# Regrouping the last group of modes alone in a fused linear-attention and spectral-mixing kernel

## The chip, the cores and the metric

The kernel runs on one core of one Trainium2 chip, as one launch. The metric is the device time of an execution in microseconds (us). Of three timed executions the median was 444.92 us (444.81, 444.92 and 445.96).

## What is computed

Two layers run one behind the other. The first is a linear attention (8 batches, 8 heads, 576 positions, head width 64) with exponential features; its result, laid out as `x` with 8 batches, 576 positions and 512 columns, feeds the second. Only the second matters for the change:

```python
X = np.fft.rfft(x, axis=1)
Xr, Xi = np.real(X[:, :64]), np.imag(X[:, :64])
Yr = einsum('bmd,mde->bme', Xr, w_r) - einsum('bmd,mde->bme', Xi, w_i)
Yi = einsum('bmd,mde->bme', Xr, w_i) + einsum('bmd,mde->bme', Xi, w_r)
y = np.fft.irfft(Yr + 1j * Yi, n=576, axis=1)   # the other frequencies are 0
u = x + y
out = u + np.maximum(u @ w_ch, 0)
```

Each of the 64 lowest frequencies (modes) has its own two 512 x 512 matrices, 134 MB in all as they stand in memory. They are read once.

## The kernel before, in words

**Stages.** For the first 310 us the attention runs, one step per batch and pair of heads, and the mode products of three quarters of the columns run between its steps. A *group* `k` (0 to 31) is a set of modes by a set of the 512 input columns. Groups 24 to 31 are the last 128 input columns; group 24+gi holds eight modes, 4·gi to 4·gi+3 and 32 above these. From group 21 on the work is in the loop that begins at line 858, the *last stage*, and everything the change touches lies there.

**Weights.** `weights(k)` issues four transfers per group from the POOL queue (line 169): two halves of `wr`, two of `wi`, 512 KB written each. A group's tiles are one of three sets (`NW = 3`), so group 31 is loaded into the tiles of group 28, once group 28 has been multiplied.

**One group in the loop** (lines 859 to 880). TensorE (PE) multiplies by `wr` (`modes_of(k, 0)`, line 438), does a piece of other work, and multiplies by `wi` (`modes_of(k, 1)`), both into one PSUM tile `psY`. VectorE (DVE) adds the sum of the earlier columns out of `Yacc` and gives `yst` (line 466): 128 rows, which are 8 modes by real and imaginary part by 8 batches. PE transposes it (line 837), DVE copies the transpose into one half of `sY` (line 838). `sY` has two halves, for an even and an odd `gi`.

**The regrouping.** The inverse transform needs, for each batch, the mode rows of that batch. When both halves of `sY` are there, `by_batch(sY, P)` picks with a column step of 8 the 32 columns of each batch: `mm_z` multiplies them by `w_ch` (line 732), `mm_r` by a unit matrix (line 738), four batches side by side in four quarters of the PE. Batches 0 to 3 go into the PSUM tile T0 and 4 to 7 into T1. Eight copies of 32 rows then put them into `zall` and `yall` (one tile, `zy`), four by ScalarE (ACT) out of T0 and four by DVE out of T1 (line 748). They are queued in a list; `regroup(n)` issues the next n pairs: two pairs at once, the other two in the next group behind its first piece of other work. Pair P fills the rows 32·P to 32·P+31 of every batch.

**The other work.** Every 128 x 512 piece of `x` is transposed (`flip_x`, line 694, copied by DVE in line 697) and multiplied by `w_ch` (`times_w`, line 705): two PSUM tiles `psW` per call, each cast by ACT into `xw` (line 707). The tag of `psW` has two buffers. Some pieces of `x` are also put into another row order (`reordered`, lines 722 and 724), through the tiles T0 and T1.

**Groups 30 and 31 before the change.** Group 30 (gi = 6) fills the even half of the last `sY` and then runs a `flip_x` and the next to last `times_w` calls. Behind the loop stand a `times_w`, the first half of group 31, the last `times_w`, `add_xw` of the first output unit, the second half of group 31, `add_x`, and then `mode_sum` in two halves. `yst` of both groups goes to `yall` by three transfers (line 893). The transposes fill the odd half of `sY`; `mm_r` for batches 0 to 3 gives batch 0's `yall` rows by a DVE copy (line 903). `mm_z` for batches 0 to 3 gives batch 0's `zall` rows by an ACT copy (line 908) and a staging tile `st0` (line 909); `mm_z` for batches 4 to 7 gives `st1`, copied by DVE. Seven transfers bring the other batches' `zall` rows from there (line 913).

**Output units.** 18 units then follow (lines 915 to 929). Each adds on PE `xw` (778) and the inverse transform of `zall` (785) into `psB`, which ACT passes through the maximum (787), and `x` (793) and the inverse transform of `yall` (799) into `psA`, which DVE adds (801). Ten units have `x` added on POOL instead (804). SP sends each out (929). PSUM tiles of odd units come from a new pool that takes the place of the stage's own.

The order of instructions on each engine is that of the program text (`tc.manual_schedule()`); engines wait for one another by semaphores.

Of the kernel before, what the change touches and what calls it, by code (L numbers as in the profile page):

```python
# [10 lines left out]
F32 = mybir.dt.float32  # L11
F32R = mybir.dt.float32r
BF16 = mybir.dt.bfloat16
# [5 lines left out]
B_, H_, S_, D_ = 8, 8, 576, 64  # L19
NMODES = 64  # L20
DMODEL = 512
# [5 lines left out]
def kernel(  # L27
# [11 lines left out]
    nc = tc.nc  # L39
# [4 lines left out]
    psum = psum_cm.__enter__()  # L44
    pw = ctx.enter_context(tc.tile_pool(name="pw", bufs=3))

    ident_b = const.tile([128, 128], BF16, name="ident_b")
# [9 lines left out]
    wchb = pers.tile([128, 4, DMODEL], BF16, name="wchb")  # L57
# [49 lines left out]

    groups = [(h, -1 - G) for h in range(2) for G in range(4)]
    groups += [(g, gi) for g in range(1, 4) for gi in range(8)]

    after = [3] * 4 + [7] * 4 + [15] * 8 + [23] * 8 + [31] * 8
    W = {}
# [333 lines left out]
    def mode_sum(k, psY, pb=None):  # L446
        g, gi = groups[k]
        if gi < 0:
            G = -1 - gi
            if g == 0:  # L450
                nc.vector.tensor_copy(Yacc[:, 2 * G:2 * G + 2, :], psY)
            else:
                nc.vector.tensor_tensor(  # L453
                    out=Yacc[:, 2 * G:2 * G + 2, :], in0=psY, in1=Yacc[:, 2 * G:2 * G + 2, :],
                    op=ALU.add)
        elif g < 3:
            nc.vector.tensor_tensor(
                out=Yacc[:, gi, :], in0=psY, in1=Yacc[:, gi, :], op=ALU.add)
        else:

            cuts = [0, DMODEL] if k < 31 else [0, DMODEL // 2, DMODEL]
            yst = []
            for a, b in zip(cuts, cuts[1:]):
                t = pb.tile([128, b - a], BF16, name="yst", tag="yst" if k < 31 else f"yst{a}",
                            bufs=2 if k < 31 else 1)
                nc.vector.tensor_tensor(out=t, in0=psY[:, a:b], in1=Yacc[:, gi, a:b], op=ALU.add)
                yst += [t[:, x:x + 128] for x in range(0, b - a, 128)]
                Yst.append((t, gi, a, b))
            return yst
# [201 lines left out]
    pb = ctx.enter_context(tc.tile_pool(name="pb", bufs=2))  # L671
# [3 lines left out]
    psum = psum_cm.__enter__()  # L675

    zy = pb.tile([128, 2, B_ + 1, DMODEL], BF16, name="zy", bufs=1)
    zall, yall = zy[:, 0], zy[:, 1]
    Yst = []
# [6 lines left out]
    def slot(b):  # L686
        return b or B_

    def flip_x():
        i = todo.pop(0)  # L690
        pt = psum.tile([128, 2, 4, 128], BF16, name="pt", tag="tr")
        for x in range(2):
            for dc in range(4):
                nc.tensor.transpose(  # L694
                    pt[:, x, dc, :], xs_all[:, i + x, dc * 128:(dc + 1) * 128], ident_b)
        sT = pb.tile([128, 2, 4, 128], BF16, name="sT", tag="sT", bufs=3)
        nc.vector.tensor_copy(sT, pt)  # L697
        ahead.append((i, sT))

    def times_w():  # L700
        i, sT = ahead.pop(0)
        for x in range(2):
            ps = psum.tile([128, DMODEL], F32, name="psW", tag="pW", bufs=2)
            for dc in range(4):
                nc.tensor.matmul(ps, lhsT=sT[:, x, dc, :], rhs=wchb[:, dc, :],  # L705
                                 start=(dc == 0), stop=(dc == 3))
            nc.scalar.copy(xw[:, i + x - N_EARLY, :], ps)  # L707
# [18 lines left out]
    def columns(sY):  # L726
        return [sY[:, dc].rearrange("p g c -> p (g c)") for dc in range(4)]

    def mm_z(ps, cols, h):
        for dc in range(4):  # L730
            for j in range(4):
                nc.tensor.matmul(ps[32 * j:32 * j + 32, :], lhsT=cols[dc][:, j + 4 * h::8],
                                 rhs=wchb[:, dc, :], start=(dc == 0), stop=(dc == 3))

    def mm_r(ps, cols, h):
        for dc in range(4):
            for j in range(4):
                nc.tensor.matmul(
                    ps[32 * j:32 * j + 32, dc * 128:(dc + 1) * 128],
                    lhsT=cols[dc][:, j + 4 * h::8], rhs=ident_b, start=True, stop=True)  # L740
# [15 lines left out]
    def regroup(n):  # L756
        for _ in range(n):
            if copies:
                copies.pop(0)()
# [71 lines left out]
                        ap=[[9 * DMODEL, 64], [5 * DMODEL, 2], [1, m * DMODEL]]),  # L831
                o[:, s, :].rearrange("p c e -> p (c e)")))

    def transposed(yst, sY, gi, pts):
        for (a, b), pt in pts:
            for dc in range(a, b):
                nc.tensor.transpose(pt[:, dc - a, :], yst[dc], ident_b)
            nc.vector.tensor_copy(sY[:, a:b, gi % 2, :], pt)

    def modes_of(k, part, psY=None):  # L840
        if part == 0:
            while issue["k"] < min(k + NW, 32):
                weights(issue["k"])
                issue["k"] += 1
            issue_weights()
        return mode_mm(k, "pY", (part,), psY)

    def piece():
        times_w()
        if todo:  # L850
            flip_x()

    issue = dict(k=k_in)
    pieces_behind = (22, 24, 26, 28, 30)
    with tc.manual_schedule():
        flip_x()
        flip_x()
        for k in range(k_out, 31):
            gi = groups[k][1]
            psY = modes_of(k, 0)  # L860
            piece()
            regroup(99)
            modes_of(k, 1, psY)
            yst = mode_sum(k, psY, pb)
            if k in pieces_behind:
                times_w()
            if yst is not None:
                if gi % 2 == 0:
                    sY = pb.tile([128, 4, 2, 128], BF16, name="sY", tag="sY")
                transposed(yst, sY, gi, (((0, 4), psum.tile([128, 4, 128], BF16, name="ptY",  # L870
                                                            tag="tr")),))
            if k in pieces_behind and todo:
                flip_x()
            if yst is not None and gi % 2 == 1:
                by_batch(sY, gi // 2)
                regroup(2)
            else:
                for tag in ("T0", "T1"):
                    if reorder:
                        reordered(tag)  # L880
        assert not todo and not copies and not reorder
        times_w()
        psY = modes_of(31, 0)
        times_w()
        assert not ahead
        u0 = units[0]
        add_xw(u0)
        modes_of(31, 1, psY)
        add_x(u0)
        yst = mode_sum(31, psY, pb)  # L890
        for m, eng in ((-2, nc.sync), (-1, nc.gpsimd), (-3, nc.sync)):
            t, gi, a, b = Yst[m]
            eng.dma_start(yall[96 + 16 * (gi - 6):112 + 16 * (gi - 6), 0:B_, a:b],
                          t)
        transposed(yst, sY, 7, [
            (dcs, psum.tile([128, 2, 128], BF16, name="ptY", tag=tag, bufs=bufs))
            for dcs, tag, bufs in (((0, 2), "tr", 1), ((2, 4), "pW", 2))])
        cols = columns(sY)
        st = [pb.tile([128, DMODEL], BF16, name=f"st{h}", bufs=1) for h in range(2)]
        rows = slice(96, 128)  # L900
        r = psum.tile([128, DMODEL], F32, name="psR", tag="tr")
        mm_r(r, cols, 0)
        nc.vector.tensor_copy(yall[rows, slot(0), :], r[0:32])
        for h in range(2):
            z = psum.tile([128, DMODEL], F32, name="psZ", tag=("pW", "pY")[h], bufs=2 - h)
            mm_z(z, cols, h)
            if h == 0:
                nc.scalar.copy(zall[rows, slot(0), :], z[0:32])
            (nc.scalar.copy, nc.vector.tensor_copy)[h](st[h], z)
        for b, eng in ((1, nc.sync), (4, nc.gpsimd), (5, nc.sync), (6, nc.gpsimd),  # L910
                       (2, nc.sync), (7, nc.gpsimd), (3, nc.gpsimd)):
            j = b % 4
            eng.dma_start(zall[rows, b, :], st[b // 4][32 * j:32 * j + 32])

        for n, u in enumerate(units):
            if n == 1:
                psum_cm.__exit__(None, None, None)
                psum = ctx.enter_context(
                    tc.tile_pool(name="psumT", bufs=1, space=bass.MemoryType.PSUM))
            output_tile(u)  # L920
            if n:
                add_xw(u)
            add_z(u)
            if n:
                add_x(u)
            spec(u)
            while leave and leave[0] <= n:
                for dst, part in units[leave.pop(0)]["dmas"]:
                    nc.sync.dma_start(dst, part)
# [30 lines left out]
```

## Time and profile before

| | |
|---|---|
| median of three executions | 444.92 us |
| profiled execution | 445.59 us |
| its span, first to last instruction | 443.8 us |
| mean granted TensorE clock | 0.879 |
| PE busy | 310.9 us (70%) |
| DVE busy | 293.7 us (66%) |
| ACT busy | 270.8 us (61%) |
| moved by the DMA engines | 97.86 MB, 221 GB/s on average |

A row of the timeline gives the start in us from the span's start, the duration in us, the engine, the line, the operation, the tile written and the tiles read, their sizes and how many instructions are merged in the row; in brackets stands the idle time before it and what ended it. PE is a matrix product, PEld the load of its stationary operand; `128*32` says that a stationary operand of 128 rows and 32 columns takes one quarter of the array. A row of the chain of waits gives the start, the duration and what the end of the program was waiting for in that stretch. A row of the table by stretches gives, for each stretch, the busy time of each engine with its number of instructions, the granted clock (1.00 is full), the busy share of the DMA engines and GB/s.

### The profile page before, as it was taken

The page shows a single profiled execution, that of the slowest core. Times are in us where ns is not written, and L with a number is a line of the kernel's source. Part 1 is how long each engine was busy: PE and PEld are TensorE (multiplying, and loading weights), DVE is VectorE, ACT ScalarE, POOL GpSimd, SP SyncE. Part 2 cuts the span into 40 slices and gives each one's busy share as a digit, 9 for nine tenths or more (in the row PEclk, how much of TensorE's full clock was granted, in tenths as well). Part 3 has the DMA queues.
Part 4 walks back from the last instruction along what each step waited for, and adds up shares of the span by engine and source line. Part 5 has one row for each costly group of instructions (what it writes and reads, how often), then busy time and mean ns, then how long its engine had stood idle before and what let it go on. Part 6 is the DMA issues. An engine that isn't in the chain of part 4 may idle for free.

```text
span 443.8 us, 11840 instructions
## 1 busy us (share of the span) xinstructions
PE 310.9 (70%) x4981; PEld 201.5 (45%) x4981; DVE 293.7 (66%) x417; ACT 270.8 (61%) x567; POOL 218.1 (49%) x303
## 2 busy tenths in 40 slices
PE   0666667775767777677453767766897776789993
PEld 0455555554555655465342544433443333344441
DVE  4778879989888687878744796664232356363783
ACT  3676687886886875688633866663363254353762
POOL 6776448585566656547534554442222222200893
PEclk9999899899896596868966787888999699889997
DMA  8999999999999999999999999999999999993598
GB/s 190 243 228 218 220 228 217 229 218 218 230 221 223 221 233 221 223 233 222 223 220 222 222 222 211 211 212 211 211 211 211 211 211 211 211 207 74 183 363 328
DMA packets 60997, 97.86 MB, mean 221 GB/s; under 512 B 3936, under 2 KB 28992, under 8 KB 60944
## 3 DMA queue, kind: packets, MB, share of 16 engines
q0 software_dynamic: 51952, 76.69, 95.9%
q1 hardware_dynamic: 8832, 20.35, 13.3%
q8 instruction: 39, 0.64, 0.5%
q10 hardware_dynamic: 160, 0.07, 0.1%
q14 instruction: 14, 0.11, 0.1%
HBM read 163.64 MB, written 9.44 MB: 390 GB/s over the span
## 4 chain that ended last, share of the span: by engine, by line
DMA 55%; DVE 18%; PE 14%; issue 4%; ACT 4%; POOL 2%; ACTq 0%; SPq 0%; DVEq 0%; POOLq 0%
DMA wi<-in_moe_w_i_dram 35%; DMA wr<-in_moe_w_r_dram 9%; DMA k<-in_k_dram 8%; DVE mkq L248 7%; DVE nd L337 2%; DVE xs_all L351 2%; ACT AA L255 2%; DVE tB L330 2%; PE psB L785 2%; PE psB L778 2%; DMA kn<-in_k_dram 2%; PE psA L799 2%; PE ptr L199 1%; POOL vaug L285 1%; DMA fs<-in_w_phi_dram 1%
## 5 line engine op out<-in xcount | busy, mean ns | idle before, releaser
L285 POOL TENSOR_TENSOR vaug<-vn,ee 128x576 bf16<-128x576 f32 x64 | 72.7, 1156 | 45.7 <-ACT ee L270 43.6
L255 ACT ACTIVATE AA<-psT 128x1024 bf16<-128x1024 f32 x64 | 62.0, 1021 | 24.9 <-PE psT L223 24.2
L169 POOL DMA_DIRECT2D wr<-in_moe_w_r_dram x48 | 29.7, 620 | 78.4 <-PE psY L438 21.0
L277 ACT ACTIVATE e<-mkq 64x4 f32<-64x4 f32 (+1 forms) x128 | 26.3, 206 | 60.1 <-DVE mkq L248 57.7
L259 ACT ACTIVATE AA<-psk 128x1024 bf16<-128x1024 f32 x64 | 61.4, 1009 | 0.0
L169 POOL DMA_DIRECT2D wi<-in_moe_w_i_dram x48 | 29.9, 625 | 45.0 <-DMA wi<-in_moe_w_i_dram 13.5
L248 DVE TENSOR_REDUCE mkq<-psk 128x8 f32<-128x1024 f32 x32 | 38.7, 1211 | 0.7 <-PE psk L214 0.7
L248 DVE TENSOR_REDUCE mkq<-psq 128x8 f32<-128x1024 f32 x32 | 38.9, 1217 | 0.4 <-PE psq L214 0.3
L438 PE MATMUL psY<-wi,XT 128*32 128x512 bf16 x192 | 19.1, 477 | 26.1 <-DMA wi<-in_moe_w_i_dram 26.1
L707 ACT CAST xw<-psW 128x512 bf16<-128x512 f32 x34 | 19.8, 586 | 25.5 <-PE psW L705 25.2
L438 PEld LDWEIGHTS <-XT 128*32 128x32 bf16 x384 | 14.6, 173 | 45.8 <-issue 23.1
L705 PE MATMUL psW<-wchb,sT 128*128 128x512 bf16 x136 | 33.3, 389 | 0.0
L205 DVE COPY kT<-ptr 128x640 bf16<-128x640 bf16 x32 | 15.7, 492 | 25.3 <-PE ptr L199 25.3
L330 DVE TENSOR_TENSOR tB<-psNB,e 128x650 f32<-128x650 f32 x32 | 26.6, 832 | 8.8 <-PE psNB L320 8.4
L320 PEld LDWEIGHTS <-AA 128*128 128x128 bf16 x640 | 28.8, 110 | 7.6 <-issue 7.1
L697 DVE COPY sT<-pt 128x1024 bf16<-128x1024 bf16 x17 | 11.8, 692 | 30.5 <-PE pt L694 30.5
L223 PE MATMUL psT<-qT,w 64*128 64x512 bf16 x64 | 15.4, 471 | 23.4 <-DVE mkq L248 23.3
L199 PE MATMUL ptr<-ident_b,k 128*128 128x128 bf16 x160 | 18.1, 259 | 19.6 <-DVE qT L205 17.7
L351 DVE TENSOR_TENSOR xs_all<-nd,rden 128x640 bf16<-128x640 f32 x32 | 30.4, 951 | 1.1
L301 PE MATMUL kvz<-vaug,AA 64*128 64x65 bf16 x1152 | 28.8, 208 | 2.3 <-DVE Yacc L453 1.5
L337 DVE TENSOR_TENSOR nd<-psNA,tB 128x650 f32<-128x650 f32 x32 | 26.7, 835 | 3.8 <-DVE tB L330 0.5
L301 PEld LDWEIGHTS <-AA 64*128 64x128 bf16 x1152 | 24.5, 106 | 6.9 <-issue 2.3
(142 smaller groups left out, 726.6 us busy)
## 6 DMA issues: line engine op xcount, KB each, us to landing
wr<-in_moe_w_r_dram POOLq DMA_DIRECT2D x62, 512.0 KB, 18.9
wi<-in_moe_w_i_dram POOLq DMA_DIRECT2D x62, 512.0 KB, 18.7
out_dram<-of SPq DMA_DIRECT2D x15, 512.0 KB, 4.7
vn<-in_v_dram SPq DMA_DIRECT2D x24, 288.0 KB, 6.0
q<-in_q_dram POOLq DMA_DIRECT2D x12, 288.0 KB, 17.4
k<-in_k_dram POOLq DMA_DIRECT2D x12, 288.0 KB, 17.6
vn<-in_v_dram SPq DMA_DIRECT2D x16, 144.0 KB, 7.0
Yacc<-in_moe_w_r_dram POOLq DMA_DIRECT2D x2, 512.0 KB, 8.7
```

The lines of the kernel that those rows point to most:

```text
L169: nc.gpsimd.dma_start(t.rearrange("p (m i) e -> p m (i e)", i=2), w[8 * gi + y:8 * gi + 8:2, g * 128:(g + 1) * 128, :].rearrange("m (p i) ...
L248: nc.vector.tensor_reduce(out=o, in_=i, axis=AX.X, op=ALU.max, apply_absolute_value=True)
L255: nc.scalar.activation(AA[:, 0, ab, 0:1024].rearrange("f (x j p) -> f j x p", j=2, p=64), st["psT"].rearrange("f j (x p) -> f j x p", p=64 ...
L259: nc.scalar.activation(AA[:, 1, ab, 0:1024].rearrange("p (c j f) -> p j c f", c=4, j=2), st["psk"], ACT.Exp, scale=sc)
L285: nc.gpsimd.tensor_tensor(out=vaug[:, ab, :, 0:64], in0=st["v"], in1=ee[:, ab, :].unsqueeze(2).to_broadcast([128, 9, D_]), op=ALU.mult,)
L301: nc.tensor.matmul(kvz[:, hh, ab * 65:(ab + 1) * 65], lhsT=AA[r, 1, ab, 128 * j:128 * j + 128], rhs=vaug[r, ab, j, :], start=(j == 0), sto ...
L320: nc.tensor.matmul(p[:, hh, 65 * c:65 * c + 65], lhsT=AA[:, 0, ab, x:x + 128], rhs=kvzF[:, hh, ab * 65:(ab + 1) * 65], start=True, stop=True,)
L330: nc.vector.tensor_tensor(out=tB, in0=st["psNB"], in1=e2.unsqueeze(3).to_broadcast([128, 2, NCH, 65]), op=ALU.mult,)
L337: nc.vector.tensor_tensor(out=nd, in0=st["psNA"], in1=st["tB"], op=ALU.add)
L351: nc.vector.tensor_tensor(out=xo, in0=nd[:, :, :, 0:64], in1=rden.to_broadcast([128, 2, NCH, 64]), op=ALU.mult,)
L438: nc.tensor.matmul(psY[32 * j:32 * j + 32, :], lhsT=XT[:, 16 + 32 * ri:48 + 32 * ri, 32 * i + 4 * gi + j], rhs=wt[ri][:, 2 * j + i, :], st ...
L705: nc.tensor.matmul(ps, lhsT=sT[:, x, dc, :], rhs=wchb[:, dc, :], start=(dc == 0), stop=(dc == 3))
```

## The change

The groups 30 and 31 change places: group 30 is now gi = 7 and group 31 gi = 6. Group 30's transpose goes to the odd half of the `sY` tile that groups 28 and 29 used, and `by_batch` runs behind it for the last 32 rows, with all eight copies issued at once. The half of it that belongs to gi = 6 holds old columns at that time, and its rows are written again behind group 31. The order in `reordered` is changed by name only: the trace of before has 20 such products (ten pieces, the last two behind group 28, at 381.1 us), and none behind group 30, so the longer tuple at group 28 adds nothing.

Group 31 is regrouped by itself. A second unit matrix `ident_q`, with its columns in another order, is made once at the start of the stage by a DVE copy. The transposes of group 31 use it, so that the 16 rows of each batch come out as 16 neighbouring columns. Four products with all 128 columns give `z` of all batches, and four products with the first 16 columns give `r` of batch 0. ACT copies batch 0's `zall` rows and then all of `z` into one staging tile; seven transfers of 16 rows follow. One transfer of `yst` fewer is issued on SP.

```diff
     groups += [(g, gi) for g in range(1, 4) for gi in range(8)]
+    groups[30:] = [(3, 7), (3, 6)]
...
+        nc.vector.tensor_copy(ident_q.rearrange("r (b c) -> r c b", b=B_),
+                              ident_b.rearrange("r (c b) -> r c b", b=B_))
...
                 by_batch(sY, gi // 2)
-                regroup(2)
+                regroup(2 if k < 30 else 99)
             else:
-                for tag in ("T0", "T1"):
+                for tag in ("T0", "T1", "T0", "T1")[:4 if k == 28 else 2]:
...
-        for m, eng in ((-2, nc.sync), (-1, nc.gpsimd), (-3, nc.sync)):
-            t, gi, a, b = Yst[m]
-            eng.dma_start(yall[96 + 16 * (gi - 6):112 + 16 * (gi - 6), 0:B_, a:b],
-                          t)
-        transposed(yst, sY, 7, [
+        rows = slice(96, 112)
+        for (t, _, a, b), eng in zip(Yst[-2:], (nc.sync, nc.gpsimd)):
+            eng.dma_start(yall[rows, 0:B_, a:b], t)
+        transposed(yst, sY, 6, [
             (dcs, psum.tile([128, 2, 128], BF16, name="ptY", tag=tag, bufs=bufs))
-            for dcs, tag, bufs in (((0, 2), "tr", 1), ((2, 4), "pW", 2))])
-        cols = columns(sY)
-        st = [pb.tile([128, DMODEL], BF16, name=f"st{h}", bufs=1) for h in range(2)]
-        rows = slice(96, 128)
-        r = psum.tile([128, DMODEL], F32, name="psR", tag="tr")
-        mm_r(r, cols, 0)
-        nc.vector.tensor_copy(yall[rows, slot(0), :], r[0:32])
-        for h in range(2):
-            z = psum.tile([128, DMODEL], F32, name="psZ", tag=("pW", "pY")[h], bufs=2 - h)
-            mm_z(z, cols, h)
-            if h == 0:
-                nc.scalar.copy(zall[rows, slot(0), :], z[0:32])
-            (nc.scalar.copy, nc.vector.tensor_copy)[h](st[h], z)
+            for dcs, tag, bufs in (((0, 2), "tr", 1), ((2, 4), "pW", 2))], ident_q)
+        r = psum.tile([16, DMODEL], F32, name="psR", tag="tr")
+        z = psum.tile([128, DMODEL], F32, name="psZ", tag="pW", bufs=2)
+        for dc in range(4):
+            nc.tensor.matmul(z, lhsT=sY[:, dc, 0, :], rhs=wchb[:, dc, :],
+                             start=(dc == 0), stop=(dc == 3))
+            nc.tensor.matmul(r[:, dc * 128:(dc + 1) * 128], lhsT=sY[:, dc, 0, 0:16],
+                             rhs=ident_b, start=True, stop=True)
+        nc.scalar.copy(zall[rows, slot(0), :], z[0:16])
+        nc.vector.tensor_copy(yall[rows, slot(0), :], r)
+        st = pb.tile([128, DMODEL], BF16, name="st", bufs=1)
+        nc.scalar.copy(st, z)
         for b, eng in ((1, nc.sync), (4, nc.gpsimd), (5, nc.sync), (6, nc.gpsimd),
                        (2, nc.sync), (7, nc.gpsimd), (3, nc.gpsimd)):
-            j = b % 4
-            eng.dma_start(zall[rows, b, :], st[b // 4][32 * j:32 * j + 32])
+            eng.dma_start(zall[rows, b, :], st[16 * b:16 * b + 16])
```

`transposed` takes the unit matrix as a new argument; every other call gives it `ident_b`.

More of the change, by code (lines that the diff above doesn't have):

```diff
@@ L832, in output_tile, with transposed @@
                 o[:, s, :].rearrange("p c e -> p (c e)")))
-    def transposed(yst, sY, gi, pts):
+    def transposed(yst, sY, gi, pts, ident):
         for (a, b), pt in pts:
             for dc in range(a, b):
-                nc.tensor.transpose(pt[:, dc - a, :], yst[dc], ident_b)
+                nc.tensor.transpose(pt[:, dc - a, :], yst[dc], ident)
             nc.vector.tensor_copy(sY[:, a:b, gi % 2, :], pt)
@@ L851, in piece @@
             flip_x()
+    ident_q = pb.tile([128, 128], BF16, name="ident_q", bufs=1)
     issue = dict(k=k_in)
@@ L870 @@
                 transposed(yst, sY, gi, (((0, 4), psum.tile([128, 4, 128], BF16, name="ptY",
-                                                            tag="tr")),))
+                                                            tag="tr")),), ident_b)
             if k in pieces_behind and todo:
```

## Prediction

> **What bounds the kernel now.** I read the table by stretches first, then the chain of waits of the last 80 us, then the timeline from 365 us on. Up to 398 us the DMA engines are busy without a break at about 211 GB/s with the weights. The chain of waits shows what ends last:
>
> ```profile
> 385.86 19.60 DMA wi<-in_moe_w_i_dram
> 405.46 0.04 issue
> 405.51 0.69 PE psY L438 x5
> ...
> 407.40 0.67 PE psR L738 x16
> 408.08 1.74 PE psZ L732 x32
> 409.81 0.54 PE psB L785 x2
> ```
>
> Until 405.46 the last weights are awaited. PE is idle before that, so whatever finishes before 405.5 is free. From 405.51 the chain runs through PE: `wi` product, transposes, regrouping, and the first output unit at 409.75 by the timeline, 4.24 us after the weights. From there PE runs without a gap to 436.06, the transfers follow, and the span ends at 443.8. From 418 to 441.6 us the DMA engines are 0.99 busy, but between 410 and 418 only 0.37: they wait for units first. So all that follows moves with the start of the first unit, one for one. I predict that start.
>
> **Part 1: group 30 is regrouped ahead of the last products.** Its 64 products stand between `flip_x` and the next to last `times_w`; before, that `times_w` began at 399.86. The rows for the same work one pair earlier, and for the casts that will now queue behind it:
>
> ```profile
> 368.13 1.09 PE L732 MATMUL psZY<-wchb,sY 128*32 128x512 bf16 x16 [0.52 <-DVE sY L838]
> ...
> 369.52 2.02 ACT L748 CAST zy<-psZY 32x1024 bf16<-32x1024 f32 x2 [4.64 <-PE psZY L738]
> ...
> 370.63 2.44 DVE L748 CAST zy<-psZY 32x1024 bf16<-32x1024 f32 x2 [2.55 <-PE psZY L738]
> ```
> ```profile
> 400.92 0.59 ACT L707 CAST xw<-psW 128x512 bf16<-128x512 f32 x1 [2.22 <-PE psW L705]
> 401.79 0.59 ACT L707 CAST xw<-psW 128x512 bf16<-128x512 f32 x1 [0.28 <-PE psW L705]
> 403.38 0.59 ACT L707 CAST xw<-psW 128x512 bf16<-128x512 f32 x1 [1.00 <-PE psW L705]
> 404.24 0.59 ACT L707 CAST xw<-psW 128x512 bf16<-128x512 f32 x1 [0.28 <-PE psW L705]
> ```
>
> The first product of the pair starts at 368.13; ACT may copy 1.39 us later, DVE 2.50 us later, and PE is through after 2.45 us. A copy takes 1.01 us on ACT and 1.22 us on DVE. All eight are now issued at once, four on each engine, ahead of the last four `xw` casts on ACT and of group 31's `yst` on DVE. Each engine takes them in that order. Hence:
>
> - by_batch starts 0.09 after the `times_w` of before, for a change of operand shape (row in part 2): PE 399.95 to 402.40; ACT's copies 401.34 + 4 x 1.006 = 405.37; DVE's 402.45 + 4 x 1.22 = 407.33.
> - `times_w` (8 products of 0.216, from 8 in 1.90 with 0.39 for the last) fills both `psW` buffers by 404.2; group 31's `wr` half, 0.62 as in 401.68 to 402.30, ends at 404.9.
> - The last `times_w` needs a `psW` buffer. Its cast waits behind ACT's copies: 405.39 + 0.59 = 405.98. So PE stands from 404.9 to 406.03, then runs 1.73 for `times_w`, 0.43 for `add_xw` and 0.09 for the change of shape, to 408.28.
> - The `wi` half, whose weights lie there since 405.46, starts at 408.28 and not at 405.51: **+2.77 us**.
>
> With `psW` buffers to spare PE would not wait, and 1.1 of this would go: that much is ACT's queue, the rest PE's own 2.45, of which its idle time of before (404.6 to 405.5) covers only a part. DVE by itself (free at 407.33, where `yst` began at 406.25) would give +1.1; behind 408.28 + 0.74 it is hidden. Were by_batch to run at half clock, as at 388.14, where ACT could start only 2.41 us after the first product, 1.0 more would be added. Bounds: +1.1 to +3.8.
>
> **Part 2: group 31 alone.** Before, 48 quarter-width products run from 407.40 to the first unit at 409.75, 2.35 us, the last 16 of them (`z` of batches 4 to 7) in the way of the unit. Now 4 full products (0.216 each) alternate with 4 of 16 columns, which stream 128 columns (0.055 each, from eight transposes 399.42 to 399.86). Side by side without loss: `z` done after 1.03. But the small ones use a quarter of the array (128 x 32) and the large ones all of it, and the trace shows a gap at such changes:
>
> ```profile
> 399.86 1.89 PE L705 MATMUL psW<-wchb,sT 128*128 128x512 bf16 x8
> ...
> 401.68 0.26 PEld L438 LDWEIGHTS <-XT 128*32 128x32 bf16 x8 [0.42 <-issue]
> ```
>
> 8 x 0.216 after 399.86 is 401.59, and the quarter-width load starts at 401.68: 0.09. Back again, `psZ` from 407.90 (32 products, four at a time, 8 x 0.216) ends at 409.63 and `psB` starts at 409.75: 0.12. I take 0.10 for each of the six changes up to the last `z` product: 1.03 + 0.60 = 1.63. Then 0.24 to ACT (408.76 to 409.00 before), its copy 0.57, and 0.06 to PE: the unit starts 2.50 after the first product, against 2.35 before: **+0.15**. Bounds: -0.45 if the changes cost nothing, +0.8 if each costs 0.2.
>
> [...]
>
> **Small parts.** `ident_q` is one DVE copy, 0.23 us as `ident_p`'s row at 101.7 us, at about 314 us, where DVE idles 2.6 us and weights bound; if not hidden, 0.23. Batch 0's `r` copy on DVE (0.68) is done before the unit has run its 0.43 of `psB`. DVE's `st` copy (0.69) goes; ACT's `st` (0.59) is ready 0.5 after the unit's start, where the two were ready 0.44 and 0.80 after. SP issues one `yst` transfer less; its first `zall` transfer and POOL's four start within 0.1 of, and 0.3 before, their old places relative to the unit. Landing in 1.9 us, batch 1's rows come some 0.1 us before their product, so 0 to +0.3. The transfers are half as large; I credit nothing. The swap of groups 30 and 31 moves equal bytes in the same order: nothing. So does the longer tuple for `reordered`.
>
> **Sum.** 2.77 + 0.15 = +2.92 us on the profiled execution, 445.59 to 448.5 (span 443.8 to 446.7, 1.8 us around it). That execution lies 0.67 over the median of 444.92, so I predict **447.8 us**. A measurement can tell about 0.3%, 1.3 us, from no change.
>
> **Rivals.**
>
> *The clock falls at the tail (0.18).* The granted clock in stretches of 3.4 us:
>
> ```profile
> 373.60:377.00 3.40, 1.47 (x15) 0.72 (x13) 3.14 (x3) 2.34 (x3) 1.22 (x2) 1.00 1.12 211
> 377.00:380.40 3.40, 2.89 (x13) 1.36 (x12) 1.11 (x2) 1.17 (x2) 0.61 (x1) 0.50 1.12 211
> 383.80:387.20 3.40, 1.61 (x20) 0.89 (x19) 1.38 (x2) 0.74 (x2) 1.05 (x2) 1.00 1.12 211
> 387.20:390.60 3.40, 2.88 (x40) 1.47 (x43) 0.42 (x1) 0.05 (x1) 0.00 (x0) 0.51 1.12 211
> ...
> 404.30:407.70 3.40, 2.43 (x24) 0.81 (x22) 1.34 (x4) 0.53 (x1) 0.00 (x0) 1.00 0.05 10
> ```
>
> Behind a stretch in which PE is busy 1.47 or 1.61 us, the next runs at half clock; behind 2.43 it does not. In the new kernel PE stands 1.1 us in the last stretch and is busy for about 2.2. Were that too little, 3.4 us of PE-bound tail run at half speed: +1.7, 449.5. 2.2 lies nearer to 2.43. [...]
>
> *Not slower: the weights hide the whole of part 1 (0.12).* If the last `wi` landed at 408.3 or later relative to group 30, the copies and casts would be over first, and part 2 alone remain: +0.15 to -0.45, 444.5 to 445.1. It decides once the landings of two groups' `wi` stand 12.7 us apart (9.94 + 2.77). The products start at 365.74, 375.68, 385.62, 395.57 and 405.51, each 9.9 after the other, which speaks against it.
>
> *Only DVE's queue counts (0.08).* Should ACT's copies end early enough for the casts (two instead of four ahead) and PE's own work fit, DVE's would still be there until 407.33: +1.1 + 0.15, 446.2. The text order has all four ahead, against it.
>
> **How the numbers follow.** The forecast has 0.62, with 446.7 to 448.7 for itself by the likelier parts of its bounds. The range goes from 446.0, with DVE's case, to 449.5, with the clock's; what is left out is the hidden case and some of the edges. Slower by over 0.3% (446.3 and more): 0.62 + 0.18 + 0.03 of the DVE case = 0.83. Within 0.3%: 0.05 of the DVE case and 0.07 of the hidden case, 0.12. Faster: 0.05, the rest of the hidden case, in which part 2 would have to gain 1.3, more than I bound it by.
>
> **What would show it.** Right: four ACT copies from about 401.3 to 405.4 with an `xw` cast right behind; PE idle from 404.9 to 406.0 with ACT as releaser; the `wi` products near 408.3, with no DMA as their releaser; 0.3 us from each full product of line 904 to the next small one; the first `psB` product near 412.7. Wrong: a `wi` product released by the DMA at 405.5, a first unit before 411, `z` products 0.27 us apart, or a unit in the middle of the tail that waits for `zall`.

## The result, and the profile after

| | before | changed |
|---|---|---|
| median | 445.50 us (6 executions, 444.81 to 446.52) | 448.19 us (6, 448.00 to 449.62) |
| profiled execution | 445.59 us | 448.20 us |
| its span | 443.8 us | 446.4 us |

The ratio is 1.0060, with a 95% interval of 1.0047 to 1.0072: the change makes the kernel slower by 2.1 to 3.2 us. In the changed file the lines named in the first part up to 838 are one higher, the loop begins at line 862, the tail of group 31 stands in lines 897 to 914 and the units in 916 to 930.

The chain of waits of the changed kernel, from group 30's regrouping to the first unit:

```profile
400.13 1.02 PE psZY L733 x16
401.15 0.27 PE psZY L739 x13
401.42 0.02 issue
401.44 1.00 ACT zy L749
...
404.50 1.01 ACT zy L749
405.51 0.02 issue
405.53 0.59 ACT xw L708
406.12 0.04 issue
406.17 1.89 PE psW L706 x8
408.05 0.43 PE psB L779 x2
408.49 0.62 PE psY L439 x7
...
412.84 0.59 PE psB L786 x2
```

Before, the chain ran through the last weights until 405.46. Now no transfer stands in it behind 395.35, where the weights of group 30 arrive: it runs through the four copies on ACT, the cast queued behind them, and the last `times_w`. The rows of ACT and PE in the timeline say the same in durations:

```profile
401.44 4.06 ACT L749 CAST zy<-psZY 32x1024 bf16<-32x1024 f32 x4 [2.97 <-PE psZY L739]
405.53 1.07 ACT L708 CAST xw<-psW 128x512 bf16<-128x512 f32 x2
```
```profile
404.26 0.69 PE L439 MATMUL psY<-wr,XT 128*32 128x512 bf16 x8
406.17 1.89 PE L706 MATMUL psW<-wchb,sT 128*128 128x512 bf16 x8 [1.22 <-ACT xw L708]
```

PE idles 1.22 us, and ACT's cast is named as what ends it. In group 31's own regrouping, 16-column products stand between the whole ones:

```profile
410.31 0.39 PE L904 MATMUL psZ<-wchb,sY 128*128 128x512 bf16 x1
410.63 0.22 PE L906 MATMUL psR<-ident_b,sY 128*16 128x128 bf16 x1
410.78 0.39 PE L904 MATMUL psZ<-wchb,sY 128*128 128x512 bf16 x1
411.10 0.22 PE L906 MATMUL psR<-ident_b,sY 128*16 128x128 bf16 x1
411.26 0.39 PE L904 MATMUL psZ<-wchb,sY 128*128 128x512 bf16 x1
```

A pair takes 0.475 us, against 0.216 + 0.055 that the two stream. The first unit's `zall` product starts at 412.84, 3.09 us later than before. From there the units run as before: the last DVE addition starts 3.07 later (439.58 against 436.51), the last packet lands about 3.0 later. The span ends 2.2 us behind the last packet before and 1.8 behind it now; these 0.4 us are not explained.

### The profile page after: what moved, and what is told of

The parts are those of the page before. It is cut to its first block, busy times and chain, and to the rows that moved or that the text cites. A ratio compares the mean times of both kernels' runs of the same rounds, so it can differ in the third digit from the quotient of the medians.

```text
span 446.4 us, 11876 instructions
## 1 busy us (share of the span) xinstructions
PE 311.7 (70%) x4987; PEld 203.9 (46%) x5005; DVE 297.3 (67%) x421; ACT 275.2 (62%) x571; POOL 217.8 (49%) x303
## 4 chain that ended last, share of the span: by engine, by line
DMA 36%; DVE 25%; PE 23%; ACT 10%; issue 4%; POOL 0%; SPq 0%; ACTq 0%; DVEq 0%; POOLq 0%
DMA wi<-in_moe_w_i_dram 20%; DVE mkq L249 9%; DMA wr<-in_moe_w_r_dram 8%; DMA k<-in_k_dram 4%; DVE nd L338 4%; DVE xs_all L352 3%; ACT AA L256 3%; PE psY L439 2%; DVE tB L331 2%; PE psNB L321 2%; PE psB L779 2%; PE psB L786 2%; PE psWe L410 2%; PE psx L380 2%; DMA kn<-in_k_dram 2%
## 5 line engine op out<-in xcount | busy, mean ns | idle before, releaser
L439 PE MATMUL psY<-wi,XT 128*32 128x512 bf16 x192 | 17.9, 451 | 24.8 <-DMA wi<-in_moe_w_i_dram 24.8
L352 DVE TENSOR_TENSOR xs_all<-nd,rden 128x640 bf16<-128x640 f32 x32 | 29.5, 921 | 1.1
L749 ACT CAST zy<-psZY 32x1024 bf16<-32x1024 f32 x16 | 16.1, 1004 | 22.6 <-PE psZY L739 22.4
L224 PE MATMUL psT<-qT,w 64*128 64x512 bf16 x64 | 14.1, 430 | 22.5 <-DVE mkq L249 22.4
```

What stands on the lines that cost most here:

```text
L352: nc.vector.tensor_tensor(out=xo, in0=nd[:, :, :, 0:64], in1=rden.to_broadcast([128, 2, NCH, 64]), op=ALU.mult,)
L439: nc.tensor.matmul(psY[32 * j:32 * j + 32, :], lhsT=XT[:, 16 + 32 * ri:48 + 32 * ri, 32 * i + 4 * gi + j], rhs=wt[ri][:, 2 * j + i, :], st ...
```

## The experiments

Profiled executions differ by 1 us in where the last groups lie, so three points are compared inside each profile: A, the start of group 30's `wi` products, which the weights release; B, the start of group 31's; C, the first unit's `zall` product. In the kernels that keep the 64 products, S is the start of these. Times are in us; the ratio is to the kernel before, timed beside each, with its 95% interval. All rows but the first two were timed over five rounds; the kernel before had medians of 445.56 to 445.69 beside them. The distances come from one profile each, and A is not quite fixed: it lies 9.9 to 10.1 us behind group 29's `wi` products, but 10.55 in "spread" and 10.18 in "spread, z first".

| kernel | A to S | S to B | A to B | B to C | A to C | median | ratio |
|---|---|---|---|---|---|---|---|
| before | | | 9.94 | 4.24 | 14.18 | | 1 |
| changed, first profile | 4.71 | 8.36 | 13.07 | 4.42 | 17.49 | 448.19 | 1.0060 (1.0047 to 1.0072) |
| changed, with the others | 4.63 | 8.35 | 12.98 | 4.43 | 17.41 | 448.27 | 1.0059 (1.0043 to 1.0075) |
| z first | 3.78 | 8.35 | 12.13 | 3.65 | 15.78 | 447.06 | 1.0035 (1.0018 to 1.0052) |
| r wide | 3.78 | 8.34 | 12.12 | 3.82 | 15.94 | 447.27 | 1.0032 (1.0017 to 1.0047) |
| spread | 4.10 | 6.66 | 10.76 | 4.68 | 15.44 | 446.65 | 1.0018 (1.0002 to 1.0035) |
| spread, z first | 5.35 | 6.64 | 11.99 | 3.71 | 15.70 | 446.02 | 1.0001 (0.9983 to 1.0020) |
| both whole | | | 10.72 | 3.79 | 14.51 | 445.54 | 1.0001 (0.9982 to 1.0019) |
| both whole, 2 | | | 10.09 | 3.63 | 13.72 | 445.49 | 0.9993 (0.9983 to 1.0003) |
| both whole, 3 | | | 11.60 | 4.79 | 16.39 | 445.91 | 1.0007 (0.9990 to 1.0025) |
| before, z first | | | 9.94 | 4.03 | 13.97 | 445.35 | 0.9996 (0.9984 to 1.0008) |

**Base.** The changed kernel once more, on the chip of the second set.

> The changed kernel itself, beside the other three on one chip, so that they have a common base: 0.6% over the kernel before, first unit 17.0 to 17.5 us behind group 30's wi products (17.49 in its first profile).

It came out so: the ratio is 1.0059, and the first unit comes 17.41 us behind A.

**z first.** What do the alternating products cost?

```diff
         for dc in range(4):
             nc.tensor.matmul(z, ...)
+        for dc in range(4):
             nc.tensor.matmul(r[:, dc * 128:(dc + 1) * 128], lhsT=sY[:, dc, 0, 0:16], ...)
```

> The changed kernel with group 31's four whole z products ahead of its four 16-column r products instead of alternating with them. If each change between a whole and a quarter-width operand costs PE 0.10 us (theory), six changes and three small products leave the path: the fourth z product starts 0.65 us after the first instead of 1.42 us, the first unit comes 0.7 to 0.8 us earlier (near 412.1 us instead of 412.84) and the whole is 0.7 us faster than the changed kernel, 447.5. If the changes cost nothing and only the small products' 0.055 us each stood in the way (rival), 0.2 us faster.

B to C falls from 4.42 to 3.65, 0.77 less. The four `z` products run in one row now, the change of shape behind them:

```profile
409.17 1.04 PE L904 MATMUL psZ<-wchb,sY 128*128 128x512 bf16 x4
410.14 0.39 PE L907 MATMUL psR<-ident_b,sY 128*16 128x128 bf16 x4
```

That is the theory's size and not the rival's 0.2. Against the changed kernel the time falls by 0.24% (1.0059 to 1.0035, on two chips), 1.1 us, with some 0.2% of uncertainty.

**r wide.** Is it the shape, or the alternation?

```diff
-        r = psum.tile([16, DMODEL], F32, name="psR", tag="tr")
+        r = psum.tile([128, DMODEL], F32, name="psR", tag="tr")
...
-            nc.tensor.matmul(r[:, dc * 128:(dc + 1) * 128], lhsT=sY[:, dc, 0, 0:16],
+            nc.tensor.matmul(r[:, dc * 128:(dc + 1) * 128], lhsT=sY[:, dc, 0, :],
...
-        nc.vector.tensor_copy(yall[rows, slot(0), :], r)
+        nc.vector.tensor_copy(yall[rows, slot(0), :], r[0:16])
```

> The changed kernel with the r products taking all 128 columns instead of 16, still alternating with the z products: more work, no change of operand shape. If the change of shape is the price (theory), a pair takes 0.27 us instead of 0.475 us and the whole is 0.5 to 0.6 us faster than the changed kernel. If it is the alternation itself, or the load of each new operand (rival), a pair stays at 0.47 us or grows and the time stays at 448.2 or rises.

The `r` products have eight times the columns, and the kernel is faster. The rows of PE are:

```profile
408.57 0.39 PE L904 MATMUL psZ<-wchb,sY 128*128 128x512 bf16 x1
408.80 0.22 PE L906 MATMUL psR<-ident_b,sY 128*128 128x128 bf16 x1
408.86 0.38 PE L904 MATMUL psZ<-wchb,sY 128*128 128x512 bf16 x1
```

With the same shape the pairs stand 0.27 to 0.29 apart, so alternation itself costs nothing: the change of shape does, 0.10 each. The rival falls. The loads of the operands show the same difference. The first row is the changed kernel's, the second that of "r wide":

```profile
410.63 0.09 PEld L906 LDWEIGHTS <-sY 128*16 128x16 bf16 x1 [0.23 <-issue]
408.58 0.10 PEld L906 LDWEIGHTS <-sY 128*128 128x128 bf16 x1
```

The narrow operand is loaded only when its own product starts, 0.32 us behind the start of the whole product ahead of it; the wide one is loaded while the product ahead of it runs, 0.22 us before its own. The time falls by 0.27%, 1.2 us, where 0.5 to 0.6 us were expected; the uncertainty is again some 0.2%.

**Spread.** Does ACT's queue hold PE, or do the 64 products?

```diff
-                regroup(2 if k < 30 else 99)
+                regroup(2)
...
         times_w()
         psY = modes_of(31, 0)
+        regroup(99)
         times_w()
-        add_xw(u0)
         modes_of(31, 1, psY)
...
         transposed(yst, sY, 6, [...], ident_q)
+        add_xw(u0)
```

> The changed kernel with the last two pairs of group 30's copies issued behind group 31's wr products, so that two xw casts come ahead of them on ACT, and the first unit's add_xw moved behind the transposes. No work is left out. If ACT's queue holds PE (theory), PE's idle time of 1.2 us before the last times_w goes, the wi products start near 406.8 us instead of 408.4 us, DVE's four copies end at 407.5 us just as yst can start, and the whole is 1.4 to 1.6 us faster than the changed kernel, 446.7. If PE's 64 extra products are the price and ACT's queue only looks late (rival), only the moved add_xw is gained, 0.4 us.

S to B falls from 8.36 to 6.66. ACT's rows show the two casts ahead of the second half of the copies, and PE's wait for ACT is gone:

```profile
400.69 2.03 ACT L749 CAST zy<-psZY 32x1024 bf16<-32x1024 f32 x2 [2.36 <-PE psZY L739]
402.76 0.59 ACT L708 CAST xw<-psW 128x512 bf16<-128x512 f32 x1
403.62 0.59 ACT L708 CAST xw<-psW 128x512 bf16<-128x512 f32 x1 [0.28 <-PE psW L706]
404.23 2.02 ACT L749 CAST zy<-psZY 32x1024 bf16<-32x1024 f32 x2
```

Of the 1.70 us, `add_xw` is 0.43 (the change of shape behind it stays, now behind `psW`); the other 1.27 are ACT's queue, as PE's 1.22 of waiting said. B to C grows by 0.26: 0.20 because `add_xw` there stands in front of the first `z` product, 0.06 because `yst` now waits for DVE's copies (0.80 instead of 0.73 us behind B). The median of 446.65 is the one expected. A to S is 4.10 here because A came late: S lies 14.65 us behind group 29's `wi` products, as in the changed kernel (14.66).

**Spread, z first.**

```diff
         for dc in range(4):
             nc.tensor.matmul(r[:, dc * 128:(dc + 1) * 128], lhsT=sY[:, dc, 0, 0:16], ...)
+        add_xw(u0)
         nc.scalar.copy(zall[rows, slot(0), :], z[0:16])
```

> The changed kernel with two xw casts ahead of group 30's last two pairs of copies, with z products ahead of r products, and with add_xw of the first unit behind these, where PE waits for the zall copy. No work is left out. If the two causes are separate (theory), their gains add: the wi products start 10.8 us after group 30's (as in the run with spread copies), the first unit 3.65 us later (as with z first), 14.4 in all against 17.5 of the changed kernel and 14.2 of the kernel before; the time is 0.6% under the changed kernel, that of the kernel before within 0.2%. If both shorten one and the same wait (rival), no more than the larger gain remains: 0.4% under the changed kernel.

S to B is 6.64 and B to C 3.71: both gains stand side by side, and the time is 0.58% under the changed kernel, where "z first" had 0.24% and "spread" 0.41%. By the times alone the 0.17% beyond "spread" is no more than the uncertainty; the two distances show it. A to B is 1.2 us longer than expected, all of it in A to S, and the 4.10 of "spread" that the expectation built on was itself short. In this profile PE's eight `psW` products took 3.05 us instead of 1.90, at a granted clock of 0.63 between 394.0 and 397.4.

**Both whole.** Without the 64 products and the eight copies; `z` goes first, as above, and `add_xw` stands where it does in "spread".

```diff
-                by_batch(sY, gi // 2)
-                regroup(2 if k < 30 else 99)
+                if k < 30:
+                    by_batch(sY, gi // 2)
+                    regroup(2)
+                else:
+                    alone(sY, 1, slice(112, 128))
...
+    def alone(sY, half, rows):
+        z = psumA.tile([128, 2, DMODEL], F32, name="psZY", tag="T0")
+        for dc in range(4):
+            nc.tensor.matmul(z[:, 0], lhsT=sY[:, dc, half, :], rhs=wchb[:, dc, :],
+                             start=(dc == 0), stop=(dc == 3))
+        st = pb.tile([128, DMODEL], BF16, name="st7", bufs=1)
+        nc.vector.tensor_copy(st, z[:, 0])
+        t = Yst[-1][0]
+        nc.sync.dma_start(yall[rows, 0:B_, :], t)
+        nc.sync.dma_start(yall[rows, slot(0), :],
+                          t.rearrange("(r b) d -> r b d", b=B_)[:, 0, :])
+        for b in range(B_):
+            nc.sync.dma_start(zall[rows, slot(b), :], st[16 * b:16 * b + 16])
```

> Group 30 is regrouped in the same way as group 31: its transposes use the other unit matrix, four whole products give z of all batches, one DVE copy brings it into a staging tile, and SP transfers bring each batch's rows and yst to their places, instead of 64 quarter-width products and eight copies; z products ahead of r products and add_xw behind the transposes as well. No work is left out. If the extra PE work and the copies are what delays the last wi products (theory), these start within 0.3 us of the weights' arrival (near 405.5 us), the first unit comes 3.6 us later, near 409.1 us, and the whole is 0.4 to 0.6 us faster than the kernel before, 445.0. If the delay is something else, or the eleven additional transfers hold up the last weights or the units (rival), the time is that of the kernel before or longer.

The delay of part 1 goes: `wi` is released by the weights again. But these come 0.8 us later behind A than in the kernel before, and the time is only that of the kernel before, as the rival had it:

```profile
406.14 0.69 PE L439 MATMUL psY<-wi,XT 128*32 128x512 bf16 x8 [0.48 <-DMA wi<-in_moe_w_i_dram]
```

That the eleven transfers hold up the weights is not shown by this. `wi` products that the weights release mostly stand 9.94 us apart, but in this same profile those of group 28 came 10.65 behind those of group 27 (375.84 and 365.19), with no added transfer beside them, and in "spread" those of group 30 came 10.55 behind those of group 29. The 10.72 here may be one more such distance.

**Both whole, 2.** The same regrouping of group 30 (its transposes with `ident_b`, so that the staging tile has the row order of `yst`), but only batch 0's rows are moved early; two transfers of 128 KB (`zall` on SP, `yall` on POOL) stand behind group 31's `yst`.

```diff
-        nc.sync.dma_start(yall[rows, 0:B_, :], t)
-        nc.sync.dma_start(yall[rows, slot(0), :],
-                          t.rearrange("(r b) d -> r b d", b=B_)[:, 0, :])
-        for b in range(B_):
-            nc.sync.dma_start(zall[rows, slot(b), :], st[16 * b:16 * b + 16])
+        for part, src in ((yall, t), (zall, st)):
+            nc.sync.dma_start(part[rows7, slot(0), :],
+                              src.rearrange("(r b) d -> r b d", b=B_)[:, 0, :])
...
         for (t, _, a, b), eng in zip(Yst[-2:], (nc.sync, nc.gpsimd)):
             eng.dma_start(yall[rows, 0:B_, a:b], t)
+        nc.sync.dma_start(zall[rows7, 0:B_, :], st7)
+        nc.gpsimd.dma_start(yall[rows7, 0:B_, :], t7)
```

> Both groups by whole products, but only batch 0's rows of group 30 are transferred while the last weights arrive; the other batches' rows go in two transfers issued behind the last wi products, and add_xw stands behind the r products. No work is left out. If the 272 KB of transfers held up the last weights in the run with both groups whole (theory; there the wi products came 10.7 us after group 30's, against 9.94 before), the distance is 10.0 again, the first unit comes 3.65 us later, 13.65 in all against 14.18 before, and the kernel is 0.5 us (0.1%) faster than the kernel before, which five rounds may not tell from none. If the weights are late for another reason, or the late transfers make a unit wait for zall or yall (rival), the distance stays at 10.7 or the gap moves into the units, and the time is that of the kernel before or more.

A to B is 10.09, as the theory asked, and A to C is 13.72, 0.46 under the kernel before. Since a distance near 10.7 also occurs without these transfers, one profile of each kernel does not show that they had held up the weights. And the third unit now waits for batch 1's rows, whose transfer is issued on SP behind the large one:

```profile
410.99 0.60 PE L779 MATMUL psB<-xw,ident_p 128*128 128x512 bf16 x2
412.15 0.61 PE L786 MATMUL psB<-zy,CI 128*128 128x512 bf16 x2 [0.56 <-DMA zy<-st]
```

The product starts 1.16 us behind the one ahead of it where 0.43 is usual, so 0.7 us are lost there. The rival's gap in the units is there. The ratio, 0.9993, can't be told from none.

**Both whole, 3.** Both large transfers issued from ACT's queue, behind the second and the fourth of the last casts.

```diff
         times_w()
+        nc.scalar.dma_start(zall[rows7, 0:B_, :], st7)
         psY = modes_of(31, 0)
         times_w()
+        nc.scalar.dma_start(yall[rows7, 0:B_, :], t7)
...
-        nc.sync.dma_start(zall[rows7, 0:B_, :], st7)
-        nc.gpsimd.dma_start(yall[rows7, 0:B_, :], t7)
```

> As the second kernel with both groups by whole products, but the two transfers of 128 KB that bring the other batches' rows of group 30 are issued from ACT's queue, one behind the second and one behind the fourth of the last xw casts, near 402 and 404.6 us. No work is left out. If the unit that waited 0.7 us for batch 1's rows did so because its transfer was queued behind the large one on SP (theory), the wait goes; the last wi products come 10.1 to 10.4 us behind group 30's, the first unit 3.65 us later, so 13.8 to 14.0 against 14.2 in the kernel before: 0.2 to 0.4 us faster than it, under what five rounds can tell. If any transfer beside the last weights costs as much as it brings (rival), the distance grows to 10.7 again and the time is that of the kernel before.

Here the expectation failed. In its profile PE waits 2.04 us for the last weights, A to B is 11.60, and the stretch from 407.70 to 411.10 has a granted clock of 0.56:

```profile
404.30:407.70 3.40, 1.36 (x12) 0.45 (x10) 0.00 (x0) 1.17 (x2) 0.00 (x0) 1.00 0.44 82
407.70:411.10 3.40, 3.34 (x16) 0.90 (x13) 1.34 (x4) 0.00 (x0) 0.56 (x1) 0.56 0.16 42
```

The columns are those of the table by stretches; the third from the end is the granted clock. The four `z` products take 1.89 instead of 1.04 us, most of what makes B to C 4.79. The third unit's wait did go: its `zall` product at 414.57 starts 0.44 us behind the one ahead of it. The two transfers are what this kernel adds ahead of the late weights, and 11.60 is longer than any other distance that the weights set in these profiles; whether all 1.66 us are theirs, one profile can't tell. Its profiled execution (447.56) lies over its median (445.91).

**Before, z first.** The kernel before, with `mm_z` for batches 0 to 3 ahead of `mm_r`:

```diff
-        mm_r(r, cols, 0)
-        nc.vector.tensor_copy(yall[rows, slot(0), :], r[0:32])
         for h in range(2):
...
             if h == 0:
                 nc.scalar.copy(zall[rows, slot(0), :], z[0:32])
+                mm_r(r, cols, 0)
+                nc.vector.tensor_copy(yall[rows, slot(0), :], r[0:32])
```

> The kernel before with one edit: z of batches 0 to 3 ahead of r of batches 0 to 3. No work is left out. If what part 2 can bring is an earlier zall copy for batch 0 (theory), this alone brings the first unit from 4.24 to about 3.95 us behind the wi products, 0.3 us, with no change of group 30; the time is that of the kernel before within 0.1%, or 0.3 us less. If the first unit waits for something else, such as the staging copies (rival), nothing moves.

B to C falls from 4.24 to 4.03, 0.2 us, without any change to group 30. The time can't be told from that of the kernel before. No version that was run is clearly faster than it.

## Why the prediction was right

The time moved by 2.67 us by the ratio (2.1 to 3.2); 2.92 were forecast. The median of 448.19 lies 0.4 above the forecast: the kernel before has a median of 445.50 over six executions, where three had shown 444.92, and the change is 0.2 smaller than forecast.

- **What bounds the kernel**: right. The first unit starts 3.09 us later and the last addition 3.07. In the eleven profiles 33.5 to 34.2 us lie between C and the end of the span, wherever C lies; the 0.4 us that the profiled execution got back at its end are within this scatter.
- **Part 1**: forecast +2.77. In the profile A to B grows by 3.13; as the weights came 0.2 earlier, B lies 2.91 later. The order of events is the one forecast: copies from 401.44 to 405.50 (401.34 to 405.37), PE's wait until 406.17 (406.03), `wi` at 408.42 (408.28). S to B was forecast as 8.33 and is 8.34 to 8.36 in four profiles. Of the 0.14 that was missing, 0.11 is in the start of the 64 products (400.06 for 399.95).
- **ACT's share of it**: the estimate that 1.1 us would go if PE did not wait for a cast is near what "spread" showed, 1.27 of its 1.70.
- **Part 2**: forecast +0.15, measured +0.18. Six changes of shape at 0.10 eat what four whole products gain; "z first" and "r wide" show it by taking them away. A pair took 0.475 us with the 16-column operand and 0.27 us with the 128-column one; why a change of shape costs 0.10 us, no run shows. The traces write the small operand as `128*16`; the quarter of the array (128 x 32) that the prediction gave it is in none of them.
- **Rivals**: the weights did not hide the work: in the changed kernel the last `wi` landed at most 19.6 us behind its issue at 385.64, at about 405.2 and 9.9 behind A. DVE's queue ended at 407.48, ahead of `yst`, as costed. The clock stayed full in the changed kernel's tail: PE was busy 2.18 of 3.40 us between 404.3 and 407.7, and the next stretch has 1.00. In "both whole, 3" PE was busy 1.36 of 3.40 us there, with 2.04 us of idle time in one piece, and the next stretch has 0.56. The 3.4 us at half clock that the rival is worked out with are those of the kernel before, 0.50 from 377.0 to 380.4 and 0.51 from 387.2 to 390.6. A threshold does not follow from stretches cut at fixed times: in "z first" PE was busy for only 1.10 us in one that full clock followed.
- **What was missed**: A to S is no constant. It was 3.78 to 5.35 us in six profiles. In the changed kernel's, the clock was 0.64 between 387.2 and 390.6, group 29's products took longer, DVE's copies of that pair ended at 397.83 and group 30's `yst` waited for them. With the clock at 1.00 in that stretch ("z first") `yst` began 1.3 us behind A instead of 2.5, and S came 13.73 us behind group 29's `wi` products instead of 14.66. The forecast took one clock for the work ahead of S, that of the one profile at hand (0.51 there). So it is partly luck that the time agrees to 0.3 us: with full clock there ("z first") S came 0.93 us earlier, and how many of the timed executions had it is not known. Part of the difference between "z first" or "r wide" and the changed kernel in the timed runs may be this, since both profiles had full clock there.

## What to carry to other kernels

Work that is moved ahead of an awaited transfer is free only as far as each in-order queue it enters is free: add up its PE time against PE's idle time, and then ask for every copy it issues what stands behind it on that engine and who waits for that. The same copies in another order (two, the two casts, two) cost 1.3 us less here than four in a row. Products with operands of different widths took less time grouped than alternating, here 0.77 us less from B to C. And one distance in one profile is weak evidence: `wi` products came 10.55 and 10.65 us behind those of the group before, instead of 9.94, where no added transfer stood beside their weights.

## What the runs showed of the hardware

A 16-column product between whole ones cost more than a 128-column one in its place, of which seven eighths of the columns are not needed: 0.475 against 0.27 us a pair. Between whole products, the load of the narrow operand did not run ahead of its own product (both started at 410.63), that of the wide one did (408.58, its product at 408.80). The stretches of half clock do not lie at the same place in each execution: between 383.8 and 387.2 PE was busy 1.10 us in "z first" and 1.61 in the kernel before, and the next stretch ran at full clock in the first and at 0.51 in the second.
